# Four dV stores split over two DMA queues, and the output rows on SyncE's queue, in a one-core attention backward

## The chip, the cores and the metric

The kernel runs on one core of a Trainium2 chip. The metric is the time of one execution on the device in microseconds (us), the median of several runs. Engines are named as in the profile: PE (TensorE matmul), PEld (its weight loads), DVE (VectorE), ACT (ScalarE), POOL (GpSimd) and SP (SyncE). SP, ACT and POOL issue DMAs; sixteen DMA engines move the bytes. L616 is line 616 of the kernel before.

## The reference

One decode step of a gated mix and its backward. Inputs are bfloat16; the K and V caches are 32 heads x 4,096 keys x 128.

```python
g = sigmoid((x * gate_w).sum(-1))
q = (x @ wq)                       # 32 heads of 128
p = softmax(q @ k_cache.T / sqrt(128))
a = (p @ v_cache) @ wo
h = x @ w1 + b1;  act = h * tanh(softplus(h));  b = act @ w2
out = g * a + (1 - g) * b
# returned: out and its gradients by x, k_cache, v_cache, wq, wo, w1, b1, w2, gate_w
```

For each head the gradients by the caches are outer products: dV is p times the gradient of the head's output, dK is the gradient of the scores times q. So the kernel reads K and V (67.1 MB) once and writes dK and dV (67.1 MB) once, with some 15 MB read and 15 MB written for the weights and their gradients.

## The kernel before

Each head's K and V stand as a tile of 128 partitions x 32 keys x 128 (`Kn`, `Vn`; 1 MB, 8,192 contiguous bytes per partition), loaded by SP's queue four heads ahead (`load_k` L107, `load_v` L112, four buffers each). PE transposes them as pairs of bf16 read as f32 (`k_pe`, `v_pe`; `tr` L515), ACT copies the transposes out (`T` L524), PE forms the scores and the products with the output's gradient (`rw` L538), DVE and ACT do the softmax and its gradient, and PE forms dq and the head's output (`rw` L631).

dV and dK are formed by DVE alone. `out_half` (L605) does half a head: `outer` (L597) writes 16 of the 32 keys per partition into an output tile `o_sb` (one DVE instruction at L598). Four buffers of `o_sb` are shared by dV and dK; the last heads use free buffers of `Kn` and `Vn` instead. After the second half SP stores the whole tile, 128 rows of 8,192 bytes, with one DMA:

```python
        if k == 1:
            nc.sync.dma_start(dst[h], o_t.pop((w, h))[:])        # L616
```

The order on every engine is written out by hand in one loop over heads 0 to 30; head 31 and the last group follow after it. Within an iteration for head h the order around the stores is

```python
        dk_out(h - 1, 1)      # second half of dK of the head before, and its store
        ...
        dv_out(h, 0)
        ...
        dv_out(h, 1)          # second half of dV, and its store
        load_k(h + KBUFS)
        load_v(h + VBUFS)
        ...
        dk_out(h, 0)
```

SP carries out its DMA issues in that order. Besides heads' tiles it loads and stores the weights in groups of heads (`wq_p` L124 and L377, `wo_g` L128 and L386) and the dense block's weights (`w1_sb`, `w2_sb`), a little of it in each iteration.

POOL does little: some memsets, the loads of b1 (L155, L156), five small moves of the dense block's hidden row (L410, L412), a product for a diagonal (`mjunk`, L479), the stores of the last rows of dw2 (L800) and of db1 (L802), and at the end the three output vectors out, dx and dgate, of five rows of 256 bytes each, which stand in `fin_rows` (copied by ACT at L919):

```python
    nc.gpsimd.dma_start(out0_rows, fin_rows[0:RC, :])            # L920 to L922
    nc.gpsimd.dma_start(out1_rows, fin_rows[RC:2 * RC, :])
    nc.gpsimd.dma_start(out9_rows, fin_rows[2 * RC:3 * RC, :])
```

Of the kernel before, what the change touches and what calls it, by code (L numbers as in the profile page):

```python
# [16 lines left out]
def kernel(  # L17
# [24 lines left out]
    nc = tc.nc  # L42
    P = 128
# [5 lines left out]
    RC = D // P  # L49
# [35 lines left out]
    out0_rows = out_0.rearrange("a b (c p) -> (a b c) p", p=P)  # L85
    out1_rows = out_1.rearrange("a b (c p) -> (a b c) p", p=P)
    out9_rows = out_9.rearrange("(c p) -> c p", p=P)
# [509 lines left out]
    def outer(dst, col4, row, a, b):  # L597
        nc.vector.tensor_tensor(  # L598
            dst[:, a:b, :].rearrange("p j (k t) -> p j k t", t=4),
            row.rearrange("p (k t) -> p k t", t=4).unsqueeze(1).to_broadcast([P, b - a, Dh // 4, 4]),  # L600
            col4[:, a:b, :].unsqueeze(2).to_broadcast([P, b - a, Dh // 4, 4]), ALU.mult)

    o_t = {}

    def out_half(w, h, dst, col4, row, k):  # L605
        hh = h % G
        if k == 0:
            if w == "k" and H - KBUFS <= h < H - 1:
                o_t[w, h] = kv_in.tile([P, J, Dh], BF16, name="Kn", tag="Kn")
            elif w == "v" and h > H - VBUFS:  # L610
                o_t[w, h] = kv_in.tile([P, J, Dh], BF16, name="Vn", tag="Vn", bufs=VBUFS)
            else:
                o_t[w, h] = outs.tile([P, J, Dh], BF16, name="o_sb", tag="o_sb")
        outer(o_t[w, h], col4, row[:, hh * Dh:(hh + 1) * Dh], k * JH, (k + 1) * JH)
        if k == 1:
            nc.sync.dma_start(dst[h], o_t.pop((w, h))[:])  # L616

    def dv_out(h, k):
        out_half("v", h, dVv, p4s[h], groups[h // G]["do_row"], k)

    def dk_out(h, k):
        if h >= 0:
            out_half("k", h, dKv, ds4s[h], groups[h // G]["qs_row"], k)
# [231 lines left out]
    g, h = NG - 1, H - 1  # L855
# [61 lines left out]
    nc.tensor.transpose(fin_ps[:], fin_bf[:], ident_bf[:])  # L917
    fin_rows = const.tile([3 * RC, P], BF16, name="fin_rows")
    nc.scalar.copy(fin_rows[:], fin_ps[:])  # L919
    nc.gpsimd.dma_start(out0_rows, fin_rows[0:RC, :])  # L920
    nc.gpsimd.dma_start(out1_rows, fin_rows[RC:2 * RC, :])
    nc.gpsimd.dma_start(out9_rows, fin_rows[2 * RC:3 * RC, :])  # L922


# [28 lines left out]
```

## Time and profile before

| What | Value |
|---|---|
| time, median of 3 runs | 405.06 us (404.75 to 405.18) |
| profiled execution | 404.96 us, span 403.2 us |
| busy PE, DVE, ACT, POOL | 305.9, 287.9, 232.4, 11.8 us |
| HBM read, written | 82.03 MB, 82.03 MB |
| DMA packets, bytes | 28,708, 164.55 MB, 408 GB/s in the mean |

The profiled execution's span runs from its first to its last instruction; the time is that of the whole execution. The page's "DMA" row gives, for 40 equal slices of the span, the mean busy share of the sixteen DMA engines in tenths. Its queue list names q1 (DMAs issued by SP), q0 (those issued by POOL) and q10 (ACT's four loads at the start); q8 and q14 fetch instructions. The chain of waits follows, from the last instruction back, what released each step.

### The profile page before, as it was taken

The numbers are of one execution on the slowest core, as the hardware profiler recorded it, in microseconds if no ns is written. First come the engines' busy times: TensorE is split into PE (matmuls) and PEld (weight loads), VectorE is DVE, ScalarE is ACT, GpSimd is POOL, SyncE is SP. The second block draws the span as 40 slices with busy tenths as digits, with TensorE's granted clock in tenths as the row PEclk, the third lists the DMA queues.
The fourth block names the chain that finished last, engine by engine and source line by source line (L and its number), as shares of the span: only waits on it lengthen the run. The fifth ranks groups of instructions, "written<-read, shape, count | busy, mean of one in ns | idle before, by whom it ended". The sixth has DMA issues, their size and how long they took to land.

```text
span 403.2 us, 7688 instructions
## 1 busy us (share of the span) xinstructions
PE 305.9 (76%) x2930; PEld 207.0 (51%) x2945; DVE 287.9 (71%) x808; ACT 232.4 (58%) x468; POOL 11.8 (3%) x29
## 2 busy tenths in 40 slices
PE   2979989787897985876887779876886977677640
PEld 1556646464565663544555447544555645464420
DVE  2217738868678875769897956896997985679780
ACT  2466757754676563753668667765767655375220
POOL 3000001000000000000001200000000000000001
PEclk9999999988999998989998997988999899889555
DMA  7999999999999999999999999999999999999894
GB/s 274 428 416 423 417 424 415 417 423 424 422 422 426 423 414 424 424 418 428 422 423 428 424 418 424 427 418 423 422 419 424 425 417 425 426 422 377 360 389 153
DMA packets 28708, 164.55 MB, mean 408 GB/s; under 512 B 2991, under 2 KB 3056, under 8 KB 12288
## 3 DMA queue, kind: packets, MB, share of 16 engines
q1 hardware_dynamic: 28256, 163.97, 98.1%
q8 instruction: 23, 0.38, 0.4%
q0 software_dynamic: 384, 0.10, 0.1%
q14 instruction: 13, 0.11, 0.1%
q10 hardware_dynamic: 32, 0.01, 0.0%
HBM read 82.03 MB, written 82.03 MB: 407 GB/s over the span
## 4 chain that ended last, share of the span: by engine, by line
DMA 42%; PE 25%; DVE 22%; ACT 6%; issue 2%; POOL 0%; POOLq 0%; SPq 0%; DVEq 0%; ACTq 0%
DMA out_dram<-o_sb 40%; PE tr L515 9%; DVE o_sb L598 9%; PE rw L538 3%; PE rw L631 3%; DVE junk L362 3%; DMA wq_p<-in_A_wq_dram 2%; PE x L555 2%; DVE wq_p L372 2%; ACT rw_sb L549 2%; ACT do_row L266 2%; PE tr L324 2%; PE do_ps L263 1%; PE h_ps L405 1%; DVE mjunk L494 1%
## 5 line engine op out<-in xcount | busy, mean ns | idle before, releaser
L524 ACT COPY T<-tr 128x512 f32<-128x512 f32 x256 | 138.0, 595 | 53.0 <-PE tr L515 38.3
L598 DVE TENSOR_TENSOR o_sb<-qs_row,ds 128x2048 bf16<-128x2048 bf16 x58 | 70.8, 1220 | 37.6 <-DMA out_dram<-o_sb 37.5
L515 PE MATMUL tr<-ident_f,Kn 128*128 128x128 f32 x512 | 85.6, 295 | 5.8 <-DVE rw L508 5.8
L515 PE MATMUL tr<-ident_f,Vn 128*128 128x128 f32 x512 | 84.5, 299 | 6.6 <-ACT T L524 6.0
L515 PEld LDWEIGHTS tr<-ident_f,Vn 128*128 128x128 f32 x512 | 63.4, 154 | 27.3 <-PE tr L515 12.1
L515 PEld LDWEIGHTS tr<-ident_f,Kn 128*128 128x128 f32 x512 | 61.1, 149 | 23.2 <-PE rw L631 14.1
L598 DVE TENSOR_TENSOR o_sb<-do_row,p 128x2048 bf16<-128x2048 bf16 x58 | 68.2, 1218 | 0.0
L549 ACT COPY rw_sb<-rw 128x512 f32<-128x512 f32 x33 | 19.4, 587 | 51.2 <-PE rw L538 49.0
L631 PE MATMUL rw<-Kn,ds 128*4 128x512 bf16 x256 | 35.9, 405 | 6.4 <-DVE ds L593 5.7
L631 PE MATMUL rw<-Vn,p 128*4 128x512 bf16 x256 | 35.9, 405 | 0.0
L567 PE MATMUL mx<-ident_f,m_s 128*128 128x128 f32 x32 | 10.1, 316 | 29.7 <-DVE m_s L563 29.6
L555 PE MATMUL x<-ident_f,rw_sb 128*128 128x128 f32 x132 | 22.5, 295 | 4.4 <-ACT rw_sb L549 1.4
L362 DVE SCALAR_TENSOR_TENSOR junk<-wq_p,dq_bc 128x512 bf16<-128x512 bf16 x35 | 23.9, 684 | 0.0
L538 PE MATMUL rw<-T,qz 128*32 128x512 bf16 x256 | 22.3, 426 | 0.0
L575 ACT ACTIVATE e_bf<-x,negM 128x32 bf16<-128x32 f32 x32 | 9.3, 292 | 22.4 <-DVE dqo L639 22.1
L567 PEld LDWEIGHTS mx<-ident_f,m_s 128*128 128x128 f32 x32 | 4.5, 142 | 34.0 <-DVE m_s L563 33.9
L538 PE MATMUL rw<-T,doz 128*32 128x512 bf16 x256 | 21.4, 411 | 0.8 <-ACT T L524 0.8
L380 ACT ACTIVATE wo_g<-da_bc,o 128x640 bf16<-128x640 bf16 x28 | 20.9, 816 | 1.2 <-PE ax_ps L350 1.2
L583 PE MATMUL mx<-zd,ones_f 128*128 128x2 f32 x64 | 11.2, 245 | 13.5 <-DVE pj L579 13.4
L555 PEld LDWEIGHTS x<-ident_f,rw_sb 128*128 128x128 f32 x132 | 14.5, 145 | 13.2 <-ACT rw_sb L549 13.2
L569 DVE TENSOR_REDUCE negM<-mx 128x1 f32<-128x128 f32 x32 | 9.2, 288 | 16.1 <-PE mx L567 16.1
L631 PEld LDWEIGHTS <-ds 128*4 128x4 bf16 x256 | 9.1, 85 | 22.2 <-DVE ds L593 11.4
(174 smaller groups left out, 367.6 us busy)
## 6 DMA issues: line engine op xcount, KB each, us to landing
out_dram<-o_sb SPq DMA_DIRECT2D x58, 1024.0 KB, 16.6
Kn<-in_A_k_cache_dram SPq DMA_DIRECT2D x32, 1024.0 KB, 16.8
Vn<-in_A_v_cache_dram SPq DMA_DIRECT2D x32, 1024.0 KB, 17.3
wq_p<-in_A_wq_dram SPq DMA_DIRECT2D x4, 1280.0 KB, 8.7
wo_g<-in_A_wo_dram SPq DMA_DIRECT2D x8, 640.0 KB, 17.6
out_dram<-wo_g SPq DMA_DIRECT2D x8, 640.0 KB, 18.3
out_dram<-wq_p SPq DMA_DIRECT2D x4, 1280.0 KB, 16.3
out_dram<-Kn SPq DMA_DIRECT2D x3, 1024.0 KB, 11.4
```

Source lines behind the costliest of these rows:

```text
L362: nc.vector.scalar_tensor_tensor(jq[:], in0=wqs[g][:, c, :], scalar=1.0, in1=groups[g]["dq_bc"][:], op0=ALU.mult, op1=ALU.mult, accum_out= ...
L380: nc.scalar.activation(wos[g][:, hh, :], da_bc[:], ACT.Copy, scale=groups[g]["o4"][:, hh:hh + 1])
L515: nc.tensor.transpose(tp[:, t, :], words[:, t * P:(t + 1) * P], ident_f[:])
L524: nc.scalar.copy(T[h][:, (3 - c) * (TB // 2):(4 - c) * (TB // 2), :], tp[:])
L538: nc.tensor.matmul(rw[32 * c:32 * (c + 1), :], lhsT=z[:, par, :, :].rearrange("p m u -> p (m u)"), rhs=Tb[:, c, par, :, :], start=first an ...
L549: nc.scalar.copy(rw_sb[h][:].rearrange("p t r -> p (t r)"), rw[:])
L555: nc.tensor.transpose(xs[h][:, 3 - j, :], t[:, j, :], ident_f[:])
L567: nc.tensor.transpose(mx[:, 0:P], dgms.pop(h)[:].to_broadcast([P, P]), ident_f[:])
L575: nc.scalar.activation(es[h][:], sd[h][0], ACT.Exp, bias=negM[:], scale=scale, accum_out=zds[h][:, 0:1])
L583: nc.tensor.matmul(mx[:, P:P + 2], lhsT=ones_f[:], rhs=zds[h][:], start=True, stop=True)
L598: nc.vector.tensor_tensor(dst[:, a:b, :].rearrange("p j (k t) -> p j k t", t=4), row.rearrange("p (k t) -> p k t", t=4).unsqueeze(1).to_br ...
L631: nc.tensor.matmul(rw[32 * c:32 * c + 4, :], lhsT=c4[:, 4 * jb:4 * jb + 16].rearrange("p (j t) -> p t j", t=4)[:, 0, :], rhs=N[:, jb:jb + ...
```

## The change

The dV stores of heads 6, 12, 18 and 24 are cut by partition into three DMAs: row 0 and rows 1 to 120 are issued by POOL, rows 121 to 127 by SP. All other stores of dV and dK stay as they are. The three output vectors are stored by SP instead of POOL.

```diff
     o_t = {}
+    LIGHT = (6, 12, 18, 24)
 
     def out_half(w, h, dst, col4, row, k):
...
         outer(o_t[w, h], col4, row[:, hh * Dh:(hh + 1) * Dh], k * JH, (k + 1) * JH)
         if k == 1:
-            nc.sync.dma_start(dst[h], o_t.pop((w, h))[:])
+            o = o_t.pop((w, h))
+            if w == "v" and h in LIGHT:
+                nc.gpsimd.dma_start(dst[h, 0:1], o[0:1])
+                nc.gpsimd.dma_start(dst[h, 1:121], o[1:121])
+                nc.sync.dma_start(dst[h, 121:P], o[121:P])
+            else:
+                nc.sync.dma_start(dst[h], o[:])
...
-    nc.gpsimd.dma_start(out0_rows, fin_rows[0:RC, :])
-    nc.gpsimd.dma_start(out1_rows, fin_rows[RC:2 * RC, :])
-    nc.gpsimd.dma_start(out9_rows, fin_rows[2 * RC:3 * RC, :])
+    nc.sync.dma_start(out0_rows, fin_rows[0:RC, :])
+    nc.sync.dma_start(out1_rows, fin_rows[RC:2 * RC, :])
+    nc.sync.dma_start(out9_rows, fin_rows[2 * RC:3 * RC, :])
```

## Prediction

> **What bounds the kernel now.** I read the page's slices first, then the DMA queues, the chain of waits, the list of waits, and last the trace's records of single DMA parts.
>
> ```profile
> DMA  7999999999999999999999999999999999999894
> ...
> q1 hardware_dynamic: 28256, 163.97, 98.1%
> q0 software_dynamic: 384, 0.10, 0.1%
> ...
> DMA 42%; PE 25%; DVE 22%; ACT 6%; issue 2%; POOL 0%; POOLq 0%; SPq 0%; DVEq 0%; ACTq 0%
> ```
>
> The sixteen DMA engines are full from the second slice to the thirty-seventh, nearly all with the queue that SP issues to (q1); POOL's queue (q0) carries 0.1 MB. So bytes and their split over the engines decide, not arithmetic. The next three are from the chain in order of time, the list of waits, and the tile `o_sb`:
>
> ```profile
> 325.88 18.48 DMA out_dram<-o_sb
> 344.46 1.23 DVE o_sb L598
> ...
> DVE o_sb L598 <- DMA out_dram<-o_sb: 37.5, 20, 4.4
> ...
> DMA to landing us min/median/max: 11.7/16.6/19.8
> ```
>
> VectorE waits 20 times for an output buffer, that is for the landing of an earlier store, the last time until 344.46. A store lands 16.6 us after its issue, although 1 MB takes about 2.5 us: about six such transfers are in every engine's ring at a time.
>
> A DMA has landed when its last engine has. The views print only that end, but the trace records all sixteen semaphore increments of a DMA. For some DMAs of SP's queue (us; first, eighth, fifteenth and sixteenth increment):
>
> ```
> issued   DMA              1st     8th     15th    16th   16th-15th
>   9.89   load of Kn      27.41   27.63   27.82   27.96     0.14
>  68.55   store of o_sb   84.57   85.28   86.91   87.03     0.12
> 136.92   store of o_sb  151.84  153.16  155.21  156.18     0.97
> 232.13   store of o_sb  243.02  245.06  247.17  249.59     2.42
> 329.75   store of o_sb  337.87  339.40  342.39  346.84     4.45
> 390.73   store of wo_g  396.94  397.02  397.83  402.16     4.33
> ```
>
> One engine falls steadily behind. Its 8 rows of a load take what the others' take (2.45 us from 357.10 to 359.55), but those of a store take longer: 2.63 us from 351.78 to 354.41, with packets of 324 to 352 ns where the others show 309. From 112 us on I find every DMA's last increment within 0.3 us of the previous one plus that DMA's packets, up to 402.16, but for two places (0.5 and 0.8 us). So this engine never idles; the kernel ends when its share ends, and its rows are the currency: 2.63/8 = 0.33 us for a dV row. The others do idle: from the landing at 366.90 to the next at 374.48 the first of them takes 7.6 us for two stores and one gap of 2.7.
>
> **The change, part by part.** Executions: the profiled one took 404.96 us, span 403.18 and 1.78 around it; the median of the runs is 405.06, 0.10 more, less than the 0.2% (0.8 us) that a measurement here can tell from no change.
>
> *The 120 rows.* Four of 32 dV stores lose 120 rows to POOL's queue: 4 x 120 x 8,192 B move from q1 to q0, on the same engines, no byte added. What matters is which engines. The trace shows this split only for POOL's stores of five rows at the end:
>
> ```profile
> 393.67 0.53 POOL L920 DMA_DIRECT2D out_dram<-fin_rows  x1 [100.69 <-ACT fin_rows L919]
> 394.19 0.52 POOL L921 DMA_DIRECT2D out_dram<-fin_rows  x1
> 394.70 0.50 POOL L922 DMA_DIRECT2D out_dram<-fin_rows  x1
> ```
>
> The packet records of q0 after 396 us are fifteen of 256 B and 81 of 4 B, which is 3 x (5 rows, 11 engines with a 4 B filler, 16 semaphore writes). Three of the fifteen, at 397.986, 398.486 and 398.986, stand inside the late engine's run of 2,048 B packets, which was then the only run left; the other twelve form four runs of three. So each DMA put its five rows on the same five engines, and the late one is among them: no turn from DMA to DMA. 120 rows dealt out in the same way are 8 on each of fifteen engines from the same start; the engine left out is the sixteenth, not one of the first five. The late engine keeps its 8 rows: 0. It could also save up to 8 (rival one).
>
> *The one row.* Nearest row: POOL's one-partition store of `dh_bc` (3,456 B), recorded as sixteen packets of 216 B, 16 ns each. So I take 8,192 B as sixteen of 512 B; by 309 ns for 8,192 B that is about 20 to 30 ns on each engine, 0.03. Upper bound: one packet on the late engine, 0.33; lower bound 0.
>
> *SP's 7 rows.* One row on each of seven engines. On the late one that costs 0.33, elsewhere 0. Traces name no engine numbers; that five rows start with a set that holds the late one speaks for seven rows doing so, if both queues count alike, and I take 0.33. ACT's five-row loads at the start bear on it only weakly: following packets back, the late engine is probably one of their five.
>
> *Two more DMAs per head.* One more semaphore packet from each on the engine, 9 ns: 0.02.
>
> Sum per light head 0 + 0.03 + 0.33 + 0.02 = 0.38, four times 1.5 us. Bounds while the late engine keeps its 8: 4 x 0.02, say 0.1 us, and 4 x (0.33 + 0.33 + 0.02) = 2.7 us. Nothing covers it, since the engine never idles, and the buffer waits up to 344.46 hand it on to compute, so all later issues shift too.
>
> *Issue and waits.* POOL's two issues cost 0.5 to 0.7 us each (0.717 for the 128-row load of L155), beside VectorE's 1.22 us halves. POOL stands waiting for the second half of dV at heads 6, 12, 18 and 24, whose stores SP now issues at 98.96, 165.89, 235.98 and 306.81. Queued behind that on POOL: the product into `mjunk` (L479, 220.55; it comes before head 18's wait in the program) and the stores of L800 and L802, which ran early at 291.88 and now come after 307; nobody reads them. SP keeps one issue there, so the loads of K and V queued behind it are issued as before. The buffer of `o_sb` comes free when all three parts have landed; the 7 rows still queue in SP's ring, so 16.6 us as before.
>
> *Output rows.* SP issues three small DMAs (0.34 us each, from 393.4) instead of POOL; they queue behind `wo_g`. The late engine moves the same three packets of 256 B, now after its last 5,120 B packet instead of between its 2,048 B ones: 0, with 0.1 either way. Should the late engine end earlier, these issues, over by 394.4, still have 2.5 us of cover before the first increment of `wo_g` at 396.94.
>
> Forecast: 404.96 + 1.5 = 406.5 us.
>
> **Rivals.**
>
> *The late engine is spared (faster).* If the one row moves POOL's start on by one engine, the 120 rows take the next fifteen and leave out the engine that got the single row. For it: that engine must be the late one; the late one is among the first five, and one row plus fifteen engines makes sixteen. Against it: the three five-row DMAs did not turn. Price: it saves 8 rows less 1 or 2, four times: 24 to 28 x 0.33 = 7.9 to 9.2 us, more than its lag of 4.3, so the fifteenth engine decides. That one lands at 397.83, 4.3 before; it idled 2.1 us in the tail (its `Vn` store landed at 380.52, 4.59 after the 375.93 of the store ahead, for 2.45 us of packets), waiting for issues that themselves waited for the late engine, and may win these back; SP's 7 rows may cost it 1.3. So 3.0 to 6.4 us, about 5: 400.0, between 398.6 and 402.0. It decides from 4 x 0.38 = 1.5 us saved on the late engine, five rows in all. The Trainium skill ("DMA: Bandwidth & Descriptors", on why a DMA increments its semaphore by 16) states such a rule: GpSimd's queue takes the largest number of engines up to 16 that divides the rows, consecutive from a round-robin cursor, with some direct copies excepted that use all sixteen, rows rounded up. By the cursor, five-row DMAs would take fifteen different engines; the trace disagrees.
>
> *No change that can be told.* The late engine is not among SP's seven and the single row is split: 4 x (0.03 + 0.02) = 0.2, so 405.2. Against it: the late engine is one of POOL's first five.
>
> **How the numbers follow.** The forecast has 0.64: its one inference, that 120 rows are dealt like five, is from the same queue and direction, but from other sizes. The spared engine has 0.25, no change 0.11. The forecast's own range is 405.8 (0.2% above the time of before) to 407.8 (the 2.7 and the median's 0.10). With no change that holds 0.75, so the range must reach into the faster case: from 399.8, which leaves out the lower part of it, to 407.8. Faster by over 0.2% is 0.25, within 0.11, slower 0.64.
>
> **What would show it.** Right: in the profile after, q0 carries about 4.1 MB (121 rows of 8,192 B, four times, and the 0.1 of before); the sixteenth increment of late DMAs lies 5 us or more behind the fifteenth at 340 us; the last increment comes at about 403.7, now of the output rows; POOL's busy time grows by 2.5 to 4 us (eight issues more, three fewer); the waits of `o_sb` stay. Per piece: the single rows as 64 packets of 512 B, or as four more of 8,192 B. Wrong: the lag shrinks by 2 us or more at each of the four heads (120 rows skip the late engine), or stays the same although the rows fall on it (then rows of q0 are free there, and the engine is bound by something other than its packets).

## The result, and the profile after

The changed kernel is slower: 408.14 us (median of 5 runs, 407.96 to 409.19) against 404.83 us for the kernel before beside it (404.75 to 405.18). The ratio is 1.0087, with a 95% interval of 1.0072 to 1.0102: 2.9 to 4.1 us lost, 3.3 between the medians. The profiled execution took 408.86 us, span 407.0.

First the page of the changed kernel, then one row of the page of before for comparison. GB/s is what the DMA engines moved in each of 40 slices.

```profile
DMA  7999999999999999999999999999999999999992
GB/s 271 429 416 425 422 416 423 414 423 424 391 404 426 424 419 426 419 416 417 413 408 420 428 419 372 398 416 424 427 422 419 424 420 416 426 415 389 404 411 96
...
q1 hardware_dynamic: 27766, 160.00, 95.4%
q0 software_dynamic: 992, 4.06, 2.7%
...
DMA 42%; PE 27%; DVE 20%; ACT 6%; issue 1%; SPq 0%; DVEq 0%; ACTq 0%
```

```profile
GB/s 274 428 416 423 417 424 415 417 423 424 422 422 426 423 414 424 424 418 428 422 423 428 424 418 424 427 418 423 422 419 424 425 417 425 426 422 377 360 389 153
```

The engines are as busy as before, and 4.06 MB went over to POOL's queue. But while busy they move less in some slices: 391 and 404 GB/s around head 6 (100 us), 372 and 398 around head 18 (245 us), where the kernel before moves 422 to 427. An engine that is busy and moves less has packets that take longer. The chain of waits in order of time and the list of waits show that VectorE still hangs on stores, until 347.57 instead of 344.46, though it waits less in total than the 37.5 us of before:

```profile
331.19 16.29 DMA out_dram<-o_sb
347.57 1.22 DVE o_sb L598
```

```profile
DVE o_sb L598 <- DMA out_dram<-o_sb: 31.4, 17, 5.7
```

The tail, in the timeline of SP's queue (start, length, what): the output rows are issued behind `wo_g`.

```profile
391.50 0.67 SPq L386 DMA_DIRECT2D out_dram<-wo_g  x1
394.17 0.28 SPq L927 DMA_DIRECT2D out_dram<-fin_rows  x1
394.50 1.03 SPq L928 DMA_DIRECT2D out_dram<-fin_rows  x1
395.58 1.04 SPq L929 DMA_DIRECT2D out_dram<-fin_rows  x1
```

The semaphore increments of the same DMAs as in the prediction (us; the issue moves, so each is named as there):

```
before: issued  after: issued  DMA       1st     8th     15th    16th   16th-15th
  9.89            10.00        Kn       27.30   27.72   28.00   28.05    0.05
 68.55            68.70        o_sb     84.65   85.27   87.27   87.55    0.27
136.92           138.52        o_sb    149.49  153.41  156.20  158.14    1.94
232.13           235.75        o_sb    245.27  248.37  253.57  254.81    1.24
329.75           335.06        o_sb    339.46  343.47  348.78  349.99    1.20
390.73           391.50        wo_g    398.13  398.34  402.35  405.12    2.77
```

The last engine ends 2.96 us later than before (405.12 for 402.16), but the fifteenth even 4.52 later (402.35 for 397.83). So nearly all engines lost time, not the late one alone, and by the slices they lost it at heads 6 and 18 above all, two of the four heads that are split (the light heads). Behind 405.12 come the three output rows, landing at 405.31, 405.50 and 405.69 on that engine.

### The profile page after: what moved, and what is told of

It reads as the page before. It is cut to its first block, busy times and chain, and to the rows that moved or that the text cites. A ratio compares the mean times of both kernels' runs of the same rounds, so it can differ in the third digit from the quotient of the medians.

```text
span 407.0 us, 7718 instructions
## 1 busy us (share of the span) xinstructions
PE 308.5 (76%) x2945; PEld 207.1 (51%) x2945; DVE 286.8 (70%) x808; ACT 232.5 (57%) x468; POOL 14.4 (4%) x34
## 3 DMA queue, kind: packets, MB, share of 16 engines
q0 software_dynamic: 992, 4.06, 2.7%
## 4 chain that ended last, share of the span: by engine, by line
DMA 42%; PE 27%; DVE 20%; ACT 6%; issue 1%; SPq 0%; DVEq 0%; ACTq 0%
DMA out_dram<-o_sb 40%; PE tr L515 10%; DVE o_sb L598 7%; PE rw L538 4%; PE rw L638 3%; DVE junk L362 2%; DMA wq_p<-in_A_wq_dram 2%; PE x L555 2%; PE q_ps L211 2%; DVE wq_p L372 2%; ACT wo_g L380 1%; ACT rw_sb L549 1%; ACT do_row L266 1%; PE tr L324 1%; PE do_ps L263 1%
## 5 line engine op out<-in xcount | busy, mean ns | idle before, releaser
L515 PE MATMUL tr<-ident_f,Vn 128*128 128x128 f32 x512 | 85.8, 303 | 11.0 <-ACT T L524 10.5
L598 DVE TENSOR_TENSOR o_sb<-qs_row,ds 128x2048 bf16<-128x2048 bf16 x58 | 70.6, 1218 | 31.4 <-DMA out_dram<-o_sb 31.4
L515 PEld LDWEIGHTS tr<-ident_f,Vn 128*128 128x128 f32 x512 | 64.7, 157 | 32.2 <-ACT T L524 12.7
L638 PE MATMUL rw<-Kn,ds 128*4 128x512 bf16 x256 | 37.2, 417 | 4.7 <-DVE ds L593 4.1
L638 PE MATMUL rw<-Vn,p 128*4 128x512 bf16 x256 | 37.2, 417 | 0.0
```

Of the source, the lines that this page charges most:

```text
L515: nc.tensor.transpose(tp[:, t, :], words[:, t * P:(t + 1) * P], ident_f[:])
L598: nc.vector.tensor_tensor(dst[:, a:b, :].rearrange("p j (k t) -> p j k t", t=4), row.rearrange("p (k t) -> p k t", t=4).unsqueeze(1).to_br ...
L638: nc.tensor.matmul(rw[32 * c:32 * c + 4, :], lhsT=c4[:, 4 * jb:4 * jb + 16].rearrange("p (j t) -> p t j", t=4)[:, 0, :], rhs=N[:, jb:jb + ...
```

## The experiments

The theories, as the expectations name them. **A**: the moved output rows cost time at the end; **B**: they don't (my forecast). **R**: a light head costs what it adds to the late engine's rows. **L**: rows of a second queue that go ahead of SP's cost time by themselves. **S**: one DMA more in SP's queue costs time. **M**: what costs is rows that stand on other engines than in a whole store. **P** and **H** divide M: the partitions in SBUF, or the addresses in HBM.

In the table, cost is the median less that of the kernel before in the same runs, with the 95% interval of the ratio less 1, times 405. Long rows are packets of 8,192 B (7,168 B where rows are cut by keys) that took over 450 ns between 98 and 375 us of the profiled execution, where 309 (272) is usual; each trace has some 12,000 such packets there.

| kernel | light heads' dV | cost, us | interval | long rows |
|---|---|---|---|---|
| before | whole | 0 | | 35 |
| changed | POOL 1, 120; SP 7; output rows on SP | 3.31 | 2.9 to 4.1 | 160 |
| e1_fin_only | whole; output rows on SP | 0.78 | 0.4 to 1.1 | 36 |
| e2_light_only | POOL 1, 120; SP 7 | 2.17 | 1.8 to 2.8 | 138 |
| e3_split_on_sp | SP 1, 120, 7 | 4.84 | 3.6 to 5.2 | 206 |
| e4_whole_on_pool | POOL 128 | 6.67 | 6.0 to 7.2 | 223 |
| e5_even_pool_sp | POOL 112; SP 16 | 0.82 | 0.6 to 1.8 | 119 |
| e6_even_on_sp | SP 112, 16 | 5.79 | 4.9 to 6.8 | 151 |
| e7_uneven_on_sp | SP 120, 8 | 4.32 | 3.6 to 4.8 | 203 |
| e8_uneven_pool_sp | POOL 120; SP 8 | 2.58 | 2.1 to 3.1 | 131 |
| e9_columns_on_sp | SP 28 keys, 4 keys of all rows | 0.57 | 0.1 to 0.8 | 29 |
| e10_columns_pool_sp | POOL 28 keys; SP 4 keys | 0.50 | 0.1 to 0.8 | 36 |
| e11_half_rows_on_sp | SP 64, 64 | 5.95 | 3.4 to 6.1 | 127 |
| e12_small_load_on_sp | whole, and a small load on SP | 0.81 | 0.4 to 1.1 | 50 |
| f1_odd_even_on_sp | SP even, odd rows | 0.20 | -0.1 to 0.6 | 26 |
| f2_shifted_rows | whole, 64 rows lower in HBM | -1.38 | -1.8 to -0.9 | 35 |
| f3_odd_even_pool_sp | POOL even; SP odd rows | 0.27 | -0.1 to 0.6 | 32 |
| f4_five_rows_more | whole, and 5 rows again | 1.53 | 1.0 to 2.0 | 29 |
| f5_one_row_more | whole, and 1 row again | -0.03 | -0.1 to 0.6 | 26 |
| f6_seven_rows_more | whole, and 7 rows again | 1.19 | 0.9 to 1.9 | 35 |

**The two parts alone (e1, e2).** e1 is the second hunk of the diff, e2 the first.

> The kernel before with only the three output stores moved to SP; no dV store is split. Theory A (the end of the trace after: the late engine lands the three five-row DMAs 0.19 us apart behind its wo_g, 405.12 to 405.69, and the span ends 0.3 us later after that than before): 0.6 to 0.9 us slower than before, 405.4 to 405.7. Theory B (my forecast's term, three packets of 256 B wherever they stand): 0 with 0.1 either way, 404.8 to 404.9.

> The change without the moved output rows. If theory A holds and the terms add: 0.6 to 0.9 us faster than the changed kernel, 407.2 to 407.5, so 2.4 to 2.7 over before. Of that, theory R (rows on the late engine: one of SP's 7, 0.38 per light head) gives 1.5; theory L (the POOL queue's rows stand beside SP's and packets get long around heads 6 and 18: 48 us more packet time in the trace after, summed over sixteen engines, of which the late engine took 1.1 to 1.5) gives the rest. R alone: 406.4. R and L: 407.3, with packet time over the usual 309 ns per row of some 130 to 150 us in sum, against 102 in the trace before.

e1 cost 0.78 us: theory A. The parts add up to 2.95 us, within the interval of the change. In e1 the late engine's `wo_g` lands at 401.92, no later than before, and behind it the three small DMAs at 402.11, 402.30 and 402.48: 0.56 us in all, though their packets take some 20 ns each. Then SP waits for the semaphores of the queues in a fixed order, 0.06 us each. In e1 eight such waits stand behind that of the last landing, and the span ends 1.35 us after it; in the trace of before three stood behind it, and the span ended 1.02 us after it: another 0.33.

e2 cost 2.17 and has 138 long rows for 35: more than R's 1.5, as R and L together had it.

**The queue or the split (e3, e4).** Output rows on POOL from here on.

```diff
-                nc.gpsimd.dma_start(dst[h, 0:1], o[0:1])
-                nc.gpsimd.dma_start(dst[h, 1:121], o[1:121])
+                nc.sync.dma_start(dst[h, 0:1], o[0:1])        # e3; the 7 rows stay
+                nc.sync.dma_start(dst[h, 1:121], o[1:121])
...
+                nc.gpsimd.dma_start(dst[h], o[:])             # e4 instead of all three
```

> As the light heads of the change, but all three pieces (1, 120 and 7 rows) go by SP's queue; output rows on POOL as before. Tells the split over engines from POOL's queue. Theory R: the late engine gets its 8 rows of the 120 and one of the 7: 1.5 us slower than before, 406.4 (up to 407.7 if the single row stands on it whole). Theory L (long packets come of a second queue whose rows jump ahead): packet time over nominal stays near the 102 us of before, so no more than R. If long packets come of the uneven split alone: as e2, 407.3.

> The dV of the four light heads stored by POOL in one DMA of 128 rows, 8 on each engine; output rows on POOL as before. No engine gets a row more or fewer. Theory R: no change, 404.9 (within 0.3). Theory L: the long packets stay, 1 to 1.5 us slower than before, 406.0 to 406.4, with packet time over nominal near 140 us.

Both expectations missed. The split without POOL's queue (e3) cost 4.84 us, twice what it cost with it, so rows get long without POOL's queue too. e4 doesn't answer its question. Where POOL alone stores a tile, the program gives its buffers out in another order, and at heads 12, 18 and 24 VectorE waits for the very store that was just issued, here POOL's of 240.05, landed at 249.88:

```profile
249.98 1.22 DVE L598 TENSOR_TENSOR o_sb<-qs_row,ds 128x2048 bf16<-128x2048 bf16 x1 [10.23 <-DMA out_dram<-o_sb]
```

Behind the waits at heads 18 and 24 the DMA engines run short of work: 209 and 330 GB/s in the slices from 256 and 328 us. e4 cuts no store and yet has 223 long rows, 174 of them after 265 us. So long rows alone are no sign of a cut; where these come from was not tried. In no later kernel does VectorE wait for a store that was just issued (the shortest of its waits for a store ends 13.4 us after that store's issue).

**Even or uneven, one queue or two (e5 to e8).**

```diff
+                nc.gpsimd.dma_start(dst[h, 0:112], o[0:112])  # e5; e6: nc.sync
+                nc.sync.dma_start(dst[h, 112:P], o[112:P])
...
+                nc.sync.dma_start(dst[h, 0:120], o[0:120])    # e7; e8: nc.gpsimd
+                nc.sync.dma_start(dst[h, 120:P], o[120:P])
```

> Light heads' dV as 112 rows by POOL (7 for each of the sixteen engines) and 16 by SP (1 for each): every engine keeps 8 rows; output rows on POOL as before; buffers of o_sb in the same order. Theory R (the late engine's added rows are the cost): no change, 405.0 within 0.3. Theory L (rows of a second queue that jump ahead of SP's cost time by themselves): 0.5 to 2 us slower, with 25 us or more of added packet time around the four heads as in the changed kernel.

> The same 112 and 16 rows, both by SP's queue. Theory R: no change, 405.0 within 0.3. Theory S (one DMA more on SP takes one of the eight semaphores that its DMAs share, so fewer bytes are in flight around the heads): a few tenths up to 1 us slower, and SP waits longer for earlier DMAs.

> Light heads' dV as 120 and 8 rows, both by SP: the 120 stand on fifteen engines, 8 each, the 8 on eight, one each. Theory R: the late engine, which is among the first seven, has 9 rows: 4 x 0.35 = 1.4 us slower, 406.4. If the 4.8 us that the split 1, 120, 7 cost on SP's queue come of uneven shares as such (engines fall out of step and packets get longer): 2.5 us or more, 407.5 or above. If they came of three DMAs in the place of one (semaphores): between, and nearer to the even split on SP.

> The change's light heads without the single row: 120 rows by POOL, 8 by SP; output rows on POOL. Theory R: one row more on the late engine at each head, 1.4 us, 406.4. If the single row's DMA is part of the cost, 0.3 us or more below the 2.17 that the light heads cost alone; else 407.1 as there.

Over two queues, the uneven split costs 1.76 us more than the even one (2.58 less 0.82): R's 1.4 fits. e8 cost no less than e2 (2.58 and 2.17), so the single row's DMA is no part of the cost. But the even split isn't free, against R's expectation, and both splits on SP's queue alone cost 4.3 us and more, the even one most, where R had nothing and S at most 1 us. The rows that an engine gets don't explain that, since e5 and e6 leave each engine its eight. Left were one DMA more (S) and the rows as such (M).

**Rows or pieces (e9 to e12).**

```diff
+                nc.sync.dma_start(dst[h, :, 0:28], o[:, 0:28])   # e9; e10: nc.gpsimd
+                nc.sync.dma_start(dst[h, :, 28:J], o[:, 28:J])
...
+                nc.sync.dma_start(dst[h, 0:64], o[0:64])         # e11
+                nc.sync.dma_start(dst[h, 64:P], o[64:P])
...
+                nc.sync.dma_start(spare[:], Kv[h][0:16, 0, 0:8]) # e12, store whole
```

> Light heads' dV cut by keys instead of by rows: all 128 rows of 7,168 B and all 128 rows of 1,024 B, both by SP. As many DMAs and as many bytes on each engine as in the even split by rows on SP (112 and 16), which cost 5.8 us; here each engine keeps the partitions that it has in a whole store. Theory M (rows dealt so that engines touch partitions or addresses that other engines use at the time make packets long): within 1 us of before, 405.0 to 405.7, and packet time near that of before. Theory S (one DMA more in SP's queue is the cost: one of eight semaphores, and what is in flight): 409 or above, as the split by rows.

> The same cut by keys, the 7,168 B rows by POOL and the 1,024 B rows by SP; output rows on POOL. To be held against the even split by rows over the two queues (0.8 us over before). Theory M: no cost, 404.8 to 405.2. Theory L (rows of a second queue that go ahead of SP's cost time by themselves): 0.5 to 1 us over before, as the split by rows.

> Light heads' dV as rows 0 to 63 and 64 to 127, both by SP, four rows on each engine from each. As many DMAs as e9, but every engine has other partitions than in a whole store. Theory M: as the other splits by rows or worse, 409 or above, with the long packets inside the two pieces. Theory S: the same as the cut by keys on SP.

> The kernel before, and behind each of the four dV stores SP issues one more DMA, a load of 16 rows of 16 B into a tile that nobody reads. No store is split. Theory S in its pure form (a DMA more in the queue takes a semaphore and a place): 3 us or more slower, as the split stores on SP. Theory M: under 0.5 us slower, 405.0 to 405.4.

This decides for M. Cut by keys, with as many DMAs and bytes as e6, the cost falls from 5.79 to 0.57 us, and no long rows are left over those of before. Of the 0.57 the packets explain about half: 272 and 46 ns for a row instead of 309, by 8 rows and 4 heads 0.3 us. The rest is again the waits at the end. With four DMAs more in SP's queue (e6, e7, e9, e11, e12, f1, f4 to f6) the last `wo_g` has another semaphore, with seven waits behind it instead of three, and the span ends 1.27 us after its landing instead of 1.02: 0.25 us of the cost of each of these kernels. e10 (0.50 us) is above what M had, with the same 0.3 for its packets, and at the lower end of L. The small load of e12 cost 0.81, more than M alone had it and far from what S needs.

**Which rows (f1 to f3).**

```diff
+                nc.sync.dma_start(dst[h, 0:P:2], o[0:P:2])       # f1; f3: nc.gpsimd
+                nc.sync.dma_start(dst[h, 1:P:2], o[1:P:2])
...
+                nc.sync.dma_start(dV_rows[h * P - 64:h * P + 64], o[:])   # f2, h > 0
```

> Light heads' dV cut into even and odd rows, 64 each, both by SP. As many DMAs, rows and bytes on each engine as in the cut into halves (5.9 us over before), but if an engine takes consecutive rows of a DMA, its four even and four odd rows are its own eight rows of a whole store again. Theory M (long packets come of rows that stand on other engines than in whole transfers): no long packets, 405.0 to 405.7. If the pieces as such (four rows, more DMAs) make packets long: 409 or above. If rows are dealt in turn, one to each engine, this cut is the one that moves them, and it is 409 or above too, while the halves would not have been.

> No store is cut; the dV stores of heads 1 to 31 are written 64 rows (512 KB) too low in HBM, head 0 stores its first 64 rows only, and the last 64 rows of head 31 are left out. Each engine reads its own eight partitions, but writes addresses that another engine uses in all other transfers. Output rows on POOL as before. Theory P (partitions in SBUF make the conflict): 404.5 to 405.2. Theory H (addresses in HBM make it): long packets in all 31 stores, 10 us slower or more.

> Light heads' even rows by POOL, odd rows by SP; output rows on POOL. The change's two queues, without added rows on any engine and without moved rows. Theory M: 404.8 to 405.4, packet time near before's. Theory L (rows of a second queue cost by themselves): 0.8 us over before, as 112 rows by POOL and 16 by SP.

Two pieces of 64 rows on SP's queue, and the only difference is which 64: halves cost 5.95 us, even and odd rows 0.20, which can't be told from nothing. The windows from 235 to 260 us (us, then busy time of PE, PEld, DVE, ACT and POOL, granted clock, DMA share, GB/s) show it around head 18, first the kernel before, then the changed kernel, e11 and f1:

```profile
235.00:260.00 25.00, 21.10 (x178) 13.86 (x174) 16.78 (x47) 17.09 (x35) 0.00 (x0) 0.86 1.02 423
```

```profile
235.00:260.00 25.00, 21.01 (x181) 13.74 (x180) 15.90 (x41) 17.74 (x38) 1.08 (x2) 0.86 1.01 391
```

```profile
235.00:260.00 25.00, 20.45 (x204) 13.11 (x204) 18.09 (x52) 18.21 (x37) 0.00 (x0) 1.00 1.02 409
```

```profile
235.00:260.00 25.00, 19.64 (x202) 13.30 (x201) 16.88 (x47) 18.36 (x37) 0.00 (x0) 1.00 1.02 423
```

The engines are busy all the time in each (1.01 to 1.02), and move 423, 391, 409 and 423 GB/s. f3, over two queues, cost 0.27 us with an interval up to 0.6, where L had 0.8: L is out. f2 moves the addresses of all dV stores and leaves the partitions: 35 long rows, as many as before. It was faster by 1.38 us, and its trace shows why: the store of head 0 has four rows fewer on each engine, and from there on the late engine stays 1.1 to 1.6 us ahead of that of before. By the medians that is 1.38/4 = 0.34 us for a row. So P fits and H does not, as far as a shift by 512 KB can tell.

The Trainium skill ("SBUF — State Buffer", section "Door 1: The DMA port swizzle") states the rule that I had not weighed: DMA reaches the 128 partitions through sixteen ports of eight partitions each, and its rate depends on how many of the ports a transfer's partitions reach. By its table rows 0 to 63 reach eight of the ports, and the even rows all sixteen. The halves and the even rows agree with that (127 and 26 long rows). But by the same table rows 0 to 111 and rows 0 to 119 reach all sixteen ports too, and the stores cut there brought 119 to 203 long rows (e5 to e8), so the number of ports that a piece reaches does not explain them. No run here shows which partitions share a port or which engine takes which row, and why such pieces make packets long stays open.

**One row more (f4 to f6).** No store is cut; rows go out a second time: f4's on five engines, f5's on one and f6's, which are SP's rows of the change, on seven, as the increments of their DMAs show.

```diff
+            if w == "v" and h in LIGHT:
+                nc.sync.dma_start(dVv[H - 1, 0:40:8], o[0:40:8])   # f4
...
+                nc.sync.dma_start(dVv[H - 1, 0:1], o[0:1])         # f5
...
+                nc.sync.dma_start(dVv[H - 1, 121:P], o[121:P])     # f6
```

> No store is cut; output rows on POOL. Behind the dV stores of the four light heads SP stores five of the rows once more (0, 8, 16, 24, 32) into the place of head 31, which that head's own store fills at the end. [...] Theory R: 4 x 0.35 = 1.4 us on the late engine, and 0.2 to 0.8 for one DMA more on SP as with the small load: 406.3 to 406.9. If the late engine is not among the five: 405.0 to 405.5.

> The same with row 0 alone, which one engine takes. If that is not the late engine: 404.9 to 405.5, which is what one more DMA on SP costs. If it is: as with five rows, 406.3 to 406.9.

> [...] Theory R alone: the same as the five rows. Theory M adds to it: 0.3 us or more above the five rows, with long packets around the heads.

R by itself: five rows 1.53 us, one row nothing, seven rows 1.19. Less the 0.25 us of the waits at the end, five and seven rows are 1.28 and 0.94, or 0.32 and 0.24 a head. So the late engine is one of the five that take five rows of SP's queue, and not the one that takes a single row: f5's row of head 24 landed at 313.61, and the late engine ended the whole store issued just before it only at 321.53. f5 is also one DMA more in SP's queue at each of the four heads, at no cost that can be told, where S needs 3 us or more: S is out beyond those 0.25 us, and 0.56 of the 0.81 us of e12 stay unexplained. Single rows from one place (f6) add no long rows: that part of M's expectation failed.

## Why the prediction was right or wrong

The direction was right, and so was the view of the bound: the engine that ends last never idles, and about 0.33 us for each row that it gets is the price. The size was wrong, 1.5 forecast and 3.3 measured. Step by step:

- **SP's 7 rows, 0.33 a head.** Right. The late engine is among the seven; f4 and f6 measured 1.28 and 0.94 us for four heads without their waits at the end, where I had 1.3.
- **The one row.** Right: the trace has 64 packets of 512 B on q0.
- **The 120 rows, 0.** This step failed. Its first half held: the engine left out is not the late one, and it does not turn from DMA to DMA. After head 6 the first increment of a DMA stands 2.1 us before the second (108.88 and 111.02), after head 12 6.0 us (176.45 and 182.47): the same engine was left out twice. But I priced rows by how many each engine gets, and put nothing for which rows stand together in a piece. In the trace of before every store is whole, so no row showed a cut one; the nearest row that I took, five small rows at the end, has hardly any bytes. Long rows went from 35 to 160. Of the 2.17 us of the light heads alone, 0.9 to 1.3 are the added row by f6 and f4, which leaves 0.9 to 1.2 for the cut; by itself (e5) the cut measured 0.82, interval 0.6 to 1.8.
- **Output rows, 0 with 0.1 either way.** Failed: 0.78 us. I counted the three packets of 256 B and not that each small DMA's completion follows the one before by 0.19 us on the late engine, nor SP's waits at the end behind the last landing (0.33). On POOL's queue the rows had landed 2.6 us before the last landing (399.54 and 402.16).
- **Issue and waits, 0.** Right in what it claimed: POOL's busy time grew by 2.6 us (11.8 to 14.4). But three statements beside it did not come true: SP's 7 rows landed after 12.1 to 15.3 us instead of 16.6, VectorE's waits for `o_sb` fell from 37.5 to 31.4 us where I had them stay, and SP's three issues at the end took 0.28, 1.03 and 1.04 us instead of 0.34 each. None of the three makes the kernel slower: the first two are gains, and the issues were over at 396.62, before any engine had ended `wo_g` (398.13).

Taken together: 0.9 to 1.3 for the rows, 0.8 for the cut and 0.8 for the output rows are 2.5 to 2.9, at the lower end of the 2.9 to 4.1 of the change; e2 and e1, which hold all three, add up to 2.95. My range ended at 407.8 because its upper bound was built from rows alone; neither failed term had a bound of its own above 0.1 us. Of what I named to look for, q0's 4.06 MB, POOL's time, the split row and the output rows as last increment came true. The last increment came at 405.69 and not at about 403.7. The lag of 5 us or more behind the fifteenth engine did not (1.20 at 350 us): the others lost time too, 4.5 us on the fifteenth, most of it room that they had. My two signs of being wrong spoke of the late engine alone and did not have that case.

The rival with a spared engine, and the rule of turning engines beside it, fell with the same engine left out twice. The rival without change fell with f4.

What stays open: why cuts by rows cost 4.3 to 6.0 us on SP's queue and under 1 us where the larger piece goes by POOL's and shares are even, with about as many long rows (e5 and e6: 119 and 151). In e5 the late engine's `wo_g` lands 0.53 us after that of before (402.69), in e6 4.40 (406.56): on two queues the late engine was spared most of the loss. Why it was, was not tried. Kernels cut by rows also scatter more: e11's six runs lie between 406.74 and 411.41, and its profile is of the shortest, so its count of long rows may be low.

No kernel beat the one before; f1, f3 and f5 equal it. f2's gain is work left out: 64 rows of dV are never written.

## What to carry to other kernels

Where a store is split over queues, cut it so that each piece still spans the partitions evenly (by columns, or every second row) and not into ranges of rows: here, on one queue, the same bytes in the same number of DMAs cost 0.2 us or 6, over two queues 0.3 us or 0.8 with even shares. Where one DMA engine sets the end, price what is added to it by rows, and what stands last by completions, each with its own measured number. A term put at nothing needs an upper bound of its own, above all where no row of the trace shows the case.

## What I had not expected of the hardware

- Two DMAs of 64 rows bring long packets if they are rows 0 to 63 and 64 to 127 (127 long rows, 409 GB/s around head 18), and none beyond the usual if they are the even and the odd rows (26, and 423 GB/s).
- Completions of small DMAs on one engine come 0.19 us apart, though their packets lie 0.02 us apart (e1).
- The waits at the end of the program cost 0.06 us each behind the last landing, so the place of the last DMA's semaphore in that order is worth 0.25 to 0.33 us here.
- One DMA engine of sixteen is slow in stores: between 130 and 345 us of the kernel before, the engine that lands last ends a dK store 2.62 us and a dV store 2.52 us after the DMA ahead of it (medians), and a load of the same size after 2.45 to 2.48. With dV 512 KB lower in HBM (f2) it is 2.62 and 2.55.
